# Weight sums, paired tiles, index arithmetic and the end of a switch: one regrouping in a mixture-of-experts stage

## The chip, the cores and the metric

The kernel runs on one core of one Trainium2 chip. The metric is the device time of a run in microseconds (us). A core has TensorE (PE) for products, VectorE (DVE), ScalarE (ACT) and GpSimd (POOL) for elementwise work, and SyncE (SP), which here starts the transfers of weights. Each engine takes its instructions in order from its own queue; engines wait for one another through semaphores. GpSimd also starts the gathers and scatters by index (DMA_INDIRECT).

## The reference

Two blocks follow one another. The first is a banded attention with position bias (4 sequences, 8 heads, 768 positions, 64 per head); the change doesn't touch it. The second routes each of the 3072 tokens to the best of 8 experts:

```python
N, D, E, F = (3072, 512, 8, 1024)
logits = x @ w_gate
expert_idx = np.argmax(logits, axis=1)
gate_w = probs[np.arange(N), expert_idx]      # softmax of the logits
for e in range(E):
    mask = expert_idx == e
    h = np.maximum(x[mask] @ w1[e], 0.0)
    out[mask] = gate_w[mask, None] * (h @ w2[e])
```

All values are float32.

## The kernel before

**The parts.** Attention and routing fill about the first 200 us. They write each token with its gate weight and number to a row of its expert in DRAM (`xs_dram`). Then come the experts, class `Experts`, called from `passes`, one expert after another. Within an engine, instructions stand in the order in which the code calls them (`manual_schedule`); the program only adds the semaphores.

**The tokens of an expert.** 256 tokens are computed as two tiles of 128 (`xg`, transposed to `xT`). Experts 0 and 1 have another full tile computed before the loop (`up_s`, `down_s`). What is left of an expert's tokens comes from `xs` and is computed in a *form*: `units(e, k)`. The form number k, 0 to 7, is known only at run time, and says which of three tiles are there: a big one of 128 tokens, a middle one of 64, a low one of 32. `tc.Switch` (L1187) branches to the code of the form on TensorE, ScalarE and VectorE and back behind it. `hint` (L1180) tells TensorE and ScalarE early where the branch will go. In this run expert 0 has a middle and a low tile, 1 and 7 a low one, 2 and 4 a big one, 3, 5 and 6 a big and a low one.

**Seven products in place of eight.** The 256 tokens are multiplied by a scheme in the manner of Strassen and Winograd: both operands are cut in 2x2 blocks, sums of blocks are formed, and seven block products replace eight. So there are four sums of weight blocks for w1 (`combine1`, tile `c1`, 128x1024 each), four for w2 (`combine2`, tile `c2`, 128x1024 each), four of the tokens (`x_combine`, tile `cx`), and sums of the hidden values (`h`, `ch`) and of the results (`UV`, `gu`, `y`). The trace calls c1 and c2 both `c`.

**One expert, in order.** Inside the form: the transposes of the remainder tiles (L1124 big, L1131 smaller) are copied by VectorE to `xsT` (L1125, L1135), and TensorE does `up_a(e, 0)`, the first four of the seven block products for chunk 0 of four chunks of hidden units. `up_sums(0)` adds partial results out of PSUM bank `u[0]`: a copy on ScalarE (L1029), a sum on VectorE (L1030). Then come the remainder's products (L1144 small, `up_s` at L853 big), `up_a` and `up_sums` of chunk 1, `up_b(0)` (the other three products of chunk 0, which are added on top in the same bank, so the bank must have been read by `up_sums` first), and the remainder's second layer (L861 big, L1168 small).

Behind the form: `gather_u` and `send_u` on GpSimd, then `up_a`, `up_b`, `up_sums` and `up_end` of the remaining chunks. `up_end(j)` makes the seven tiles that the second layer needs of chunk j. Then `down_a` and `down_b` (L1066, L1075), with the next expert's `combine1` on VectorE under them, `x_in` (transposes L999 of the next expert's tokens, copies L1000 on VectorE and L1001 on ScalarE), `x_combine`, and the scaled outputs `y_out`. The last things before the next form are `combine_w2(e + 1)` (one sum on VectorE, L976, three on GpSimd, L974, L975, L977) and `meta_u(e + 1)` (L1106 to L1110, VectorE: gate weights and token numbers of the remainder, as tiles of 128x3). For two experts, `judge` puts a few more small operations there; for expert 2 it reads a result from bank `t[0]`, where the next transposes go (L1279).

**Weights** are fetched two experts ahead by SyncE into two buffers (`w[e % 2]`).

## Time and profile before

| | |
|---|---|
| Time, median of 3 runs | 636.07 us (634.67 to 636.08) |
| Profiled execution | 632.8 us |
| Mean granted clock of TensorE | 0.93 |
| Experts loop, from the first form to the last product | about 216 to 613 us |
| TensorE busy, 303.6 to 346 us (expert 2) | 30.0 of 42.4 us, granted clock 0.84 |
| TensorE busy, 390 to 417 us | 25.7 of 27 us, granted clock 1.00 |

Parts of the profile speak of different things. The busy line gives each engine's share of the span. The waits say which engine stood idle before which line, and what ended the idle time. The timeline lists instructions in order of time: start, duration, engine, line, operation, tiles, and in brackets the idle time before. The windows give busy time in stretches, with the clock that TensorE was granted (PEclk, a share of full speed). A branch isn't listed in the timeline, and the time it takes stands as idle time that "issue" ended.

### The profile page before, as it was taken

What the parts mean: (1) busy time and instruction counts of PE and PEld (TensorE: products, weight loads), DVE (VectorE), ACT (ScalarE), POOL (GpSimd) and SP (SyncE); (2) the same over time, 40 slices, a digit from 0 to 9 for tenths busy, and PEclk for the clock granted to TensorE, in tenths of its full rate; (3) what the DMA queues carried; (4) which work ended last, traced back from release to release, by engine and by line L of the source; (5) the groups of instructions that cost most, each with busy time, mean ns of one, the idle gap of its engine ahead of it and who ended that gap; (6) DMA issues with size and microseconds to landing.
All of it is one profiled execution on the core that took longest, in us unless ns stands there. A gap on an engine that the chain in (4) does not pass through costs nothing. (4 is left out here: it accounts for less than half of the span.)

```text
span 632.8 us, 13136 instructions
## 1 busy us (share of the span) xinstructions
PE 528.5 (84%) x5329; PEld 443.3 (70%) x5329; DVE 337.3 (53%) x796; ACT 139.9 (22%) x286; POOL 202.8 (32%) x204
## 2 busy tenths in 40 slices
PE   6899899899899889679389689959959995996870
PEld 5788688688687559559287576947948784794860
DVE  5567467458556426918714921870781394176330
ACT  3645254254321111102011111201211110020110
POOL 4201401401405741750811522180181134135110
PEclk9999999899899989989789979989988997997995
DMA  9989899899403304515403601540451261000000
GB/s 184 205 186 232 231 250 224 232 242 210 151 3 106 119 4 160 169 53 201 144 19 106 212 35 34 201 145 26 156 179 35 80 218 68 11 20 36 6 35 3
DMA packets 99342, 78.04 MB, mean 123 GB/s; under 512 B 80054, under 2 KB 80056, under 8 KB 99200
## 3 DMA queue, kind: packets, MB, share of 16 engines
q1 hardware_dynamic: 90368, 56.63, 35.0%
q0 software_dynamic: 8000, 19.77, 9.2%
q8 instruction: 56, 0.92, 0.6%
q14 instruction: 86, 0.70, 0.4%
q10 hardware_dynamic: 832, 0.02, 0.1%
HBM read 63.54 MB, written 14.73 MB: 124 GB/s over the span
## 5 line engine op out<-in xcount | busy, mean ns | idle before, releaser
L372 DVE TENSOR_TENSOR p<-sp,other 128x1024 f32<-128x1024 f32 x40 | 47.5, 1221 | 50.6 <-PE sp L358 48.7
L1030 DVE TENSOR_TENSOR uv<-uv,u 128x256 f32<-128x256 f32 x32 | 13.4, 419 | 110.8 <-ACT uv L1029 100.8
L853 PE MATMUL d<-xsT,w 128*128 128x128 f32 x320 | 42.3, 300 | 19.9 <-DVE xsT L1125 19.9
L853 PEld LDWEIGHTS d<-xsT,w 128*128 128x128 f32 x320 | 41.4, 215 | 22.3 <-DVE xsT L1125 20.3
L785 POOL DMA_INDIRECT xg<-xs_dram,grow x16 | 24.4, 1524 | 88.1 <-issue 84.2
L1144 PE MATMUL u<-w,xsT 128*32 128x256 f32 (+1 forms) x208 | 23.4, 566 | 31.5 <-DVE xsT L1135 31.5
L861 PE MATMUL d<-w,hsT 128*128 128x512 f32 x112 | 49.6, 593 | 0.1
L1023 PE MATMUL u<-cx,c 128*128 128x128 f32 x384 | 48.8, 277 | 0.0
L1066 PE MATMUL d<-c,ch 128*128 128x256 f32 x192 | 46.7, 379 | 0.0
L1023 PEld LDWEIGHTS u<-cx,c 128*128 128x128 f32 x384 | 46.3, 195 | 0.0
L1029 ACT COPY uv<-u 128x256 f32<-128x256 f32 x32 | 11.9, 372 | 151.3 <-PE u L1023 145.3
L379 ACT ACTIVATE p<-p 128x1024 f32<-128x1024 f32 (+1 forms) x48 | 44.6, 977 | 2.1 <-DVE p L372 2.0
L358 PE MATMUL sp<-qt,kt 64*128 64x128 f32 x448 | 41.3, 293 | 1.2 <-DVE kt L244 1.2
L300 POOL COPY ka<-kt 128x384 f32<-128x384 f32 x16 | 8.2, 510 | 105.8 <-DVE den_all L423 102.8
L785 POOL DMA_INDIRECT xs<-xs_dram,grow x24 | 24.3, 1014 | 54.1 <-PE d L853 37.1
L1066 PEld LDWEIGHTS d<-c,ch 128*128 128x128 f32 x192 | 36.5, 190 | 5.0
L1144 PEld LDWEIGHTS u<-w,xsT 128*32 128x32 f32 (+1 forms) x208 | 8.8, 151 | 43.0 <-DVE xsT L1135 32.5
L387 PE MATMUL po<-p,vt 128*64 128x128 f32 x448 | 37.1, 274 | 0.0
L861 PEld LDWEIGHTS d<-w,hsT 128*128 128x128 f32 x112 | 20.6, 190 | 23.4 <-issue 23.4
L358 PEld LDWEIGHTS sp<-qt,kt 64*128 64x128 f32 x448 | 34.1, 204 | 3.3 <-ACT qt L242 1.6
L398 PE MATMUL pr<-p,one_in 128*32 128x128 f32 x704 | 28.5, 278 | 8.7 <-issue 7.9
L793 POOL DMA_INDIRECT out_dram<-ys,to_u x8 | 8.2, 1019 | 78.7 <-DVE yu L1171 46.9
(238 smaller groups left out, 1138.3 us busy)
## 6 DMA issues: line engine op xcount, KB each, us to landing
w<-in_moe_w_dram SPq DMA_DIRECT2D x24, 1024.0 KB, 5.0
w<-in_moe_w_dram SPq DMA_DIRECT2D x16, 512.0 KB, 6.3
raw_q<-in_q_dram SPq DMA_DIRECT2D x24, 256.0 KB, 4.6
raw_k<-in_k_dram SPq DMA_DIRECT2D x24, 256.0 KB, 4.4
vt<-in_v_dram SPq DMA_DIRECT2D x24, 256.0 KB, 5.8
va<-vt SPq DMA_DIRECT2D x16, 192.0 KB, 5.6
va<-vt SPq DMA_DIRECT2D x16, 64.0 KB, 5.2
xs_dram<-xr,slot_i POOLq DMA_INDIRECT x24
```

Source lines behind the costliest of these rows:

```text
L358: nc.tensor.matmul(sp[:, a, j, t, :], lhsT=kt[r, m, :], rhs=qts[n][r, m, :], start=True, stop=True, skip_group_check=True)
L372: nc.vector.tensor_tensor(z, sc, bi, ALU.add)
L379: nc.scalar.activation(z, z, AF.Exp)
L387: nc.tensor.matmul(po[D * a:D * a + D, m, :], lhsT=vt[:, 2 * m + a, :], rhs=ps[n][m // 2][:, a, m % 2, t, :], start=(x == 0), stop=(x == l ...
L398: nc.tensor.matmul(pr[GW * m:GW * m + GW, 0, :], lhsT=one_in[:, a, :], rhs=ps[n][m // 2][:, a, m % 2, t, :], start=(x == 0), stop=False, s ...
L785: nc.gpsimd.indirect_dma_start(out=dst.bitcast(I32), out_offset=None, in_=xs_dram[:], in_offset=bass.IndirectOffsetOnAxis(ap=idx, axis=0), ...
L853: nc.tensor.matmul(ph[:, i, :], lhsT=self.w[e % 2][0][:, c, ts(half * HF + i, P)], rhs=xT[:, c, :], start=(c == 0), stop=(c == NDC - 1), s ...
L861: nc.tensor.matmul(py[:].rearrange("p a b -> p (a b)"), lhsT=self.hsT[:, f, :], rhs=self.w[e % 2][1][:, f, :], start=(f == 0), stop=(f == ...
L1023: nc.tensor.matmul(self.u[j][:, r, :], lhsT=lhs(k), rhs=rhs(k), start=first, stop=True, skip_group_check=True)
L1030: nc.vector.tensor_tensor(uv[:], uv[:], self.u[j][:, 2:4, :], ADD)
L1066: nc.tensor.matmul(self.half(i, j), lhsT=lhs, rhs=rhs, start=(f == 0 and j == 0), stop=True, skip_group_check=True)
L1144: nc.tensor.matmul(ph[n * g:n * g + n, :], lhsT=xm[:, c, cols[s]], rhs=w1t[:, c, ts(g, m)], start=(c == 0), stop=(c == NDC - 1), skip_grou ...
```

## The change

Five things are regrouped in the experts' loop; the same sums and products are computed.

1. All four sums of w2 blocks go to VectorE and to other places: three into the expert's own form (behind `up_sums(0)` and `up_b(0)`), the fourth under `down_a`. `combine_w2` at the end of the expert before is gone.
2. The sums of hidden values are done for pairs of chunks in one operation (`up_22`, `h_combine`), for which `h`, `ch` and `uv` are laid out anew; the order of operations in the scheme changes a little with it.
3. The index work is moved to GpSimd: `meta_u`, and the token numbers and gates in `x_in`.
4. Chunk 2's first products and sums (`up_a(e, 2)`, `up_sums(2)`) move from behind the form to its end.
5. Copies out of PSUM change engines: the big remainder tile and both halves of `xT` are copied by ScalarE. The scaling `gated` is split off `down_sums` and comes after `x_in`. Two of `x_combine`'s sums become one operation.

The core of the diff:

```diff
         def combine2(self, e):
-            w = self.w[e % 2][1]
-            return list(self.right([self.c2[:, i] for i in range(4)], ...
-        def combine_w2(self, e):
-            c = self.combine2(e)
-            c[2](nc.vector)
-            for i in (0, 1, 3):
-                c[i](nc.gpsimd)
+            yield lambda: nc.vector.tensor_tensor(c[:, 0], b12, b11, SUB)
+            yield lambda: nc.vector.tensor_tensor(c[:, 1], b22, c[:, 0], SUB)
+            yield lambda: nc.vector.tensor_tensor(c[:, 2], b12, b22, SUB)
+            yield lambda: nc.vector.tensor_tensor(c[:, 3], b21, c[:, 1], SUB)
...
         def x_in(self, e):
-            nc.vector.tensor_copy(out=self.xT[:, :, 0:P], in_=self.t[0][:])
-            nc.scalar.copy(self.xT[:, :, P:2 * P], self.t[1][:])
-            nc.vector.tensor_tensor(self.to[e % 2][:], ... ALU.bitwise_or)
-            nc.vector.tensor_copy(out=self.gate[e % 2][:], in_=self.xg[:, :, DM])
+            for t in range(2):
+                nc.scalar.copy(self.xT[:, :, ts(t, P)], self.t[t][:])
+            nc.gpsimd.tensor_tensor(self.to[e % 2][:], ... ADD)
+            nc.gpsimd.tensor_copy(out=self.gate[e % 2][:], in_=self.xg[:, :, DM])
...
+        def up_22(self, i):
+            j, h = slice(2 * i, 2 * i + 2), self.h[:, 2]
+            nc.vector.tensor_tensor(h[:, j, :], self.uv[:, j, 0, :], self.uv[:, j, 1, :], ADD)
+            nc.scalar.activation(h[:, j, :], h[:, j, :], AF.Relu)
         def up_end(self, j):
-            nc.vector.tensor_tensor(h[:, 1:3, :], ... b[:, 1:4:2, :], ADD)
-            nc.vector.tensor_scalar(h[:, 0, :], b[:, 0, :], 0.0, None, MAX)
-            nc.scalar.activation(h[:, 2, :], h[:, 2, :], AF.Relu)
-            nc.vector.scalar_tensor_tensor(c[:, 0, :], h[:, 1, :], 0.0, h[:, 3, :], MAX, ADD)
-            nc.vector.tensor_tensor(c[:, 1, :], c[:, 0, :], h[:, 0, :], SUB)
-            nc.vector.scalar_tensor_tensor(c[:, 2, :], h[:, 1, :], 0.0, h[:, 0, :], MAX, SUB)
-            nc.vector.tensor_tensor(c[:, 3, :], h[:, 2, :], c[:, 1, :], SUB)
+            nc.vector.tensor_tensor(self.h[:, 1:4:2, j, :], ... b[:, 1:4:2, :], ADD)
+            nc.vector.tensor_scalar(self.h[:, 0, j, :], b[:, 0, :], 0.0, None, MAX)
+        def h_combine(self, i):
+            nc.scalar.activation(h[:, 1], h[:, 1], AF.Relu)
+            nc.vector.scalar_tensor_tensor(h[:, 4], h[:, 3], 0.0, h[:, 2], MAX, ADD)
+            nc.vector.scalar_tensor_tensor(c[:, 0:2], h[:, 3:5], 0.0, ... MAX, SUB)
+            nc.vector.tensor_tensor(c[:, 2], h[:, 1], c[:, 1], SUB)
...
         def units(self, e, k):
-                nc.vector.tensor_copy(out=self.xsT[0][:], in_=self.t[0][:])
+                nc.scalar.copy(self.xsT[0][:], self.t[0][:])
...
             self.up_sums(0)
+            next(c2)()
...
             self.up_sums(1)
+            self.up_22(0)
...
             self.up_b(e, 0)
+            next(c2)()
+            next(c2)()
...
+            self.up_a(e, 2)
+            self.up_sums(2)
...
         def passes(self, judge):
                 self.send_u(e)
-                self.up_a(e, 2)
-                self.up_sums(2)
                 self.up_b(e, 1)
                 self.up_end(0)
+                self.up_end(1)
+                self.h_combine(0)
                 self.up_a(e, 3)
                 self.up_sums(3)
+                self.up_22(1)
                 self.up_b(e, 2)
-                for j in (1, 2):
-                    self.up_end(j)
+                self.up_end(2)
                 self.up_b(e, 3)
                 self.up_end(3)
+                self.h_combine(1)
                 self.down_a(e)
+                list(self.combine2(e))[3]()
...
-                    self.combine_w2(e + 1)
                     self.meta_u(e + 1)
```

`meta_u` is the same arithmetic on GpSimd, with the conversion to whole numbers as an operation of its own.

More of the change, by code (lines that the diff above doesn't have):

```diff
@@ L877, in begin @@
             self.cx = T([P, 4, HD, P], "cx")
-            self.h = T([P, HF, 4, P], "h")
-            self.ch = T([P, HF, 4, P], "ch")
-            self.uv = [T([P, 2, P], f"uv{i}") for i in range(HF)]
+            self.h = T([P, 5, HF, P], "h")
+            self.ch = T([P, 3, HF, P], "ch")
+            self.uv = T([P, HF, 2, P], "uv")
             self.UV = T([P, 2, HM], "UV")
@@ L970, in combine1 @@
             yield lambda: nc.vector.tensor_tensor(c[:, 3], a12, c[:, 1], SUB)
-        def right(self, c, b11, b12, b21, b22, sign=1):
-            yield lambda eng: eng.tensor_tensor(c[0], b12, b11, SUB)
-            yield lambda eng: eng.tensor_tensor(c[1], b22, c[0], SUB)
-            yield lambda eng: eng.tensor_tensor(c[2], *((b22, b12) if sign > 0 else (b12, b22)), SUB)
-            yield lambda eng: eng.tensor_tensor(c[3], b21, c[1], SUB)
-        def combine2(self, e):
-            w = self.w[e % 2][1]
-            return list(self.right([self.c2[:, i] for i in range(4)],
-                                   *(w[:, HF * k:HF * k + HF, HM * j:HM * j + HM]
-                                     for k in range(2) for j in range(2)), sign=-1))
-        def combine_w2(self, e):
-            c = self.combine2(e)
-            c[2](nc.vector)
-            for i in (0, 1, 3):
-                c[i](nc.gpsimd)
+        def combine2(self, e):
+            w, c = self.w[e % 2][1], self.c2
+            b11, b12, b21, b22 = (w[:, HF * k:HF * k + HF, HM * j:HM * j + HM]
+                                  for k in range(2) for j in range(2))
+            yield lambda: nc.vector.tensor_tensor(c[:, 0], b12, b11, SUB)
+            yield lambda: nc.vector.tensor_tensor(c[:, 1], b22, c[:, 0], SUB)
+            yield lambda: nc.vector.tensor_tensor(c[:, 2], b12, b22, SUB)
+            yield lambda: nc.vector.tensor_tensor(c[:, 3], b21, c[:, 1], SUB)
         def gather_x(self, e):
@@ L999, in x_in @@
                     nc.tensor.transpose(self.t[t][:, c, :], self.xg[:, t, ts(c, P)], ident[:])
-            nc.vector.tensor_copy(out=self.xT[:, :, 0:P], in_=self.t[0][:])
-            nc.scalar.copy(self.xT[:, :, P:2 * P], self.t[1][:])
-            nc.vector.tensor_tensor(self.to[e % 2][:], self.xg[:, :, DM + 1].bitcast(I32),
-                                    self.inv_i[:, e, :], ALU.bitwise_or)
-            nc.vector.tensor_copy(out=self.gate[e % 2][:], in_=self.xg[:, :, DM])
-        def x_combine(self):
-            for fn in self.right([self.cx[:, i] for i in range(4)],
-                                 *(self.xT[:, HD * k:HD * k + HD, P * j:P * j + P]
-                                   for k in range(2) for j in range(2))):
-                fn(nc.vector)
@@ L1014, in up_a @@
-        def up_a(self, e, j):
-            w, c = self.w[e % 2][0], self.c1
-            f = ts(j, P)
-            first = True
-            for r, lhs, rhs in ((0, lambda k: w[:, k, f], lambda k: self.xT[:, k, 0:P]),
-                                (2, lambda k: c[:, 1, k, f], lambda k: self.cx[:, 1, k, :]),
-                                (1, lambda k: c[:, 0, k, f], lambda k: self.cx[:, 0, k, :]),
-                                (3, lambda k: c[:, 2, k, f], lambda k: self.cx[:, 2, k, :])):
+            for t in range(2):
+                nc.scalar.copy(self.xT[:, :, ts(t, P)], self.t[t][:])
@@ new lines, in x_in @@
+            nc.gpsimd.tensor_tensor(self.to[e % 2][:], self.xg[:, :, DM + 1].bitcast(I32),
+                                    self.inv_i[:, e, :], ADD)
+            nc.gpsimd.tensor_copy(out=self.gate[e % 2][:], in_=self.xg[:, :, DM])
+        def x_combine(self):
+            x, c = self.xT, self.cx
+            nc.vector.tensor_tensor(c[:, 0:2], x[:, :, P:2 * P].rearrange("p (k c) t -> p k c t", k=2),
+                                    x[:, 0:HD, :].rearrange("p c (j t) -> p j c t", j=2), SUB)
+            nc.vector.tensor_tensor(c[:, 2], x[:, HD:NDC, P:2 * P], c[:, 0], SUB)
+            nc.vector.tensor_tensor(c[:, 3], x[:, HD:NDC, 0:P], c[:, 2], SUB)
@@ L1022, in up_a, with products @@
+        def products(self, bank, terms, first):
+            for r, lhs, rhs in terms:
                 for k in range(HD):
-                    nc.tensor.matmul(self.u[j][:, r, :], lhsT=lhs(k), rhs=rhs(k), start=first, stop=True,
+                    nc.tensor.matmul(bank[:, r, :], lhsT=lhs(k), rhs=rhs(k), start=first, stop=True,
                                      skip_group_check=True)
                     first = False
-        def up_sums(self, j):
-            uv = self.uv[j]
-            nc.scalar.copy(uv[:], self.u[j][:, 0:2, :])
-            nc.vector.tensor_tensor(uv[:], uv[:], self.u[j][:, 2:4, :], ADD)
-            nc.vector.tensor_tensor(self.h[:, j, 3, :], uv[:, 0, :], uv[:, 1, :], ADD)
-            nc.scalar.activation(self.h[:, j, 3, :], self.h[:, j, 3, :], AF.Relu)
@@ L1034, in up_b, with up_a @@
-        def up_b(self, e, j):
-            w, c = self.w[e % 2][0], self.c1
-            f, f2 = ts(j, P), ts(HF + j, P)
-            for r, lhs, rhs in ((0, lambda k: w[:, HD + k, f], lambda k: self.xT[:, HD + k, 0:P]),
-                                (1, lambda k: c[:, 3, k, f], lambda k: self.xT[:, HD + k, P:2 * P]),
-                                (3, lambda k: w[:, HD + k, f2], lambda k: self.cx[:, 3, k, :])):
-                for k in range(HD):
-                    nc.tensor.matmul(self.u[j][:, r, :], lhsT=lhs(k), rhs=rhs(k), start=False, stop=True,
-                                     skip_group_check=True)
+        def up_a(self, e, j):
+            w, c, x, f = self.w[e % 2][0], self.c1, self.xT, ts(j, P)
+            self.products(self.u[j], (
+                (0, lambda k: w[:, k, f], lambda k: x[:, k, 0:P]),
+                (3, lambda k: c[:, 0, k, f], lambda k: self.cx[:, 0, k, :]),
+                (1, lambda k: c[:, 2, k, f], lambda k: self.cx[:, 1, k, :]),
+                (2, lambda k: c[:, 1, k, f], lambda k: self.cx[:, 2, k, :])), True)
@@ new lines, in up_b @@
+        def up_b(self, e, j):
+            w, c, x, f = self.w[e % 2][0], self.c1, self.xT, ts(j, P)
+            self.products(self.u[j], (
+                (0, lambda k: w[:, HD + k, f], lambda k: x[:, HD + k, 0:P]),
+                (3, lambda k: c[:, 3, k, f], lambda k: x[:, HD + k, P:2 * P]),
+                (1, lambda k: w[:, HD + k, ts(HF + j, P)], lambda k: self.cx[:, 3, k, :])), False)
+        def up_sums(self, j):
+            uv = self.uv[:, j]
+            nc.scalar.copy(uv, self.u[j][:, 0:2, :])
+            nc.vector.tensor_tensor(uv, uv, self.u[j][:, 2:4, :], ADD)
@@ L1044, in up_end @@
+        def up_22(self, i):
+            j, h = slice(2 * i, 2 * i + 2), self.h[:, 2]
+            nc.vector.tensor_tensor(h[:, j, :], self.uv[:, j, 0, :], self.uv[:, j, 1, :], ADD)
+            nc.scalar.activation(h[:, j, :], h[:, j, :], AF.Relu)
         def up_end(self, j):
-            h, c, b = self.h[:, j], self.ch[:, j], self.u[j]
-            nc.vector.tensor_tensor(h[:, 1:3, :], self.uv[j][:, 0:1, :].to_broadcast([P, 2, P]),
+            b = self.u[j]
+            nc.vector.tensor_tensor(self.h[:, 1:4:2, j, :], self.uv[:, j, 0:1, :].to_broadcast([P, 2, P]),
@@ new lines, in h_combine @@
+        def h_combine(self, i):
+            h, c = (t[:, :, 2 * i:2 * i + 2, :].rearrange("p q j t -> p q (j t)") for t in (self.h, self.ch))
+            nc.scalar.activation(h[:, 1], h[:, 1], AF.Relu)
+            nc.vector.scalar_tensor_tensor(h[:, 4], h[:, 3], 0.0, h[:, 2], MAX, ADD)
+            nc.vector.scalar_tensor_tensor(c[:, 0:2], h[:, 3:5], 0.0,
+                                           h[:, 0:1].to_broadcast([P, 2, 2 * P]), MAX, SUB)
+            nc.vector.tensor_tensor(c[:, 2], h[:, 1], c[:, 1], SUB)
@@ L1061, in down_a @@
             for f in range(HF):
-                for i, j, lhs, rhs in ((0, 0, self.h[:, f, 0, :], w[:, f, 0:HM]),
-                                       (0, 1, self.ch[:, f, 0, :], self.c2[:, 0, f, :]),
-                                       (1, 0, self.ch[:, f, 1, :], self.c2[:, 1, f, :]),
-                                       (1, 1, self.ch[:, f, 2, :], self.c2[:, 2, f, :])):
+                for i, j, lhs, rhs in ((0, 0, self.h[:, 0, f, :], w[:, f, 0:HM]),
+                                       (0, 1, self.h[:, 4, f, :], self.c2[:, 0, f, :]),
+                                       (1, 0, self.ch[:, 1, f, :], self.c2[:, 1, f, :]),
+                                       (1, 1, self.ch[:, 0, f, :], self.c2[:, 2, f, :])):
                     nc.tensor.matmul(self.half(i, j), lhsT=lhs, rhs=rhs, start=(f == 0 and j == 0),
@@ L1070, in down_b @@
             w = self.w[e % 2][1]
-            for i, j, lhs, rhs in ((0, 1, lambda f: self.ch[:, f, 3, :], lambda f: w[:, HF + f, HM:DM]),
-                                   (0, 0, lambda f: self.h[:, f, 2, :], lambda f: w[:, HF + f, 0:HM]),
-                                   (1, 1, lambda f: self.h[:, f, 3, :], lambda f: self.c2[:, 3, f, :])):
+            for i, j, lhs, rhs in ((0, 1, lambda f: self.ch[:, 2, f, :], lambda f: w[:, HF + f, HM:DM]),
+                                   (0, 0, lambda f: self.h[:, 1, f, :], lambda f: w[:, HF + f, 0:HM]),
+                                   (1, 1, lambda f: self.h[:, 2, f, :], lambda f: self.c2[:, 3, f, :])):
                 for f in range(HF):
@@ L1081, in down_sums, with gated @@
             nc.vector.tensor_tensor(flat(self.UV), flat(self.UV), flat(self.d[1]), ADD)
+        def gated(self, e):
             for t in range(2):
@@ L1105, in meta_u @@
             f = self.to_f
-            nc.vector.tensor_copy(out=f[:], in_=self.xs[:, :, DM + 1].bitcast(I32))
+            nc.gpsimd.tensor_copy(out=f[:], in_=self.xs[:, :, DM + 1].bitcast(I32))
             for i in (1, 2):
-                nc.vector.tensor_scalar(f[:, i:i + 1], f[:, i:i + 1], float(2 * i), None, MUL)
-            nc.vector.tensor_tensor(self.to_u[e % 2][:], f[:], self.inv_u[:, e, :], ADD)
-            nc.vector.tensor_copy(out=self.gate_u[e % 2][:], in_=self.xs[:, :, DM])
+                nc.gpsimd.tensor_scalar(f[:, i:i + 1], f[:, i:i + 1], float(2 * i), None, MUL)
+            nc.gpsimd.tensor_tensor(f[:], f[:], self.inv_u[:, e, :], ADD)
+            nc.gpsimd.tensor_copy(out=self.to_u[e % 2][:], in_=f[:])
+            nc.gpsimd.tensor_copy(out=self.gate_u[e % 2][:], in_=self.xs[:, :, DM])
         def send_u(self, e):
@@ L1116, in units @@
         def units(self, e, k):
+            c2 = self.combine2(e)
             big, mid, low = k >> 2, k >> 1 & 1, k & 1
@@ L1211, in passes @@
                     self.x_in(e + 1)
+                self.gated(e)
                 self.down_b(e)
@@ L1269 @@
         ex.scatter(ex.ys[1][:], ex.tos[:, 1:2])
-        ex.combine_w2(0)
         ex.meta_u(0)
```

## The prediction

> **What bounds the kernel now.** I read the page for the busy shares, then TensorE's waits, then the timeline around one of them, then the granted clock there.

> ```profile
> span 632.8 us, 13136 instructions
> PE 528.5 (84%) x5329; PEld 443.3 (70%) x5329; DVE 337.3 (53%) x796; ACT 139.9 (22%) x286; POOL 202.8 (32%) x204
> ```

> TensorE is the bound: 84% busy. The chain of waits holds only the last scatter and explains nothing, so the question is what TensorE's missing 16% waits for. Its waits from 205 us on (engine, line, releaser: total us, times, longest):

> ```profile
> PE u L1144 <- DVE xsT L1135: 31.5, 5, 7.9
> PE d L853 <- DVE xsT L1125: 19.9, 2, 12.3
> PE t L1124 <- issue: 8.4, 2, 8.1
> PE u L1023 <- issue: 5.0, 3, 2.9
> ```

> Some 60 us are lost at one place: the start of each of the eight forms, before the first product that needs a transposed remainder tile copied by VectorE. In the timeline the gaps are 4.04, 6.91, 12.35, 8.09, 7.58, 7.87, 6.58, 6.14 = 59.6 us for experts 0 to 7. Expert 3's is named "issue", but the transposes there wait for bank t0, which VectorE reads for L1279 behind the same work. Expert 6's start (start, duration, engine, line):

> ```profile
> 519.51 0.48 DVE L1093 SCALAR_TENSOR_TENSOR y<-d,gate,gu 128x256 f32<-128x256 f32 x1 [0.38 <-PE d L1075]
> 519.91 2.80 DVE L976 TENSOR_TENSOR c<-w 128x1024 f32<-128x1024 f32 x1
> 521.69 3.21 POOL L975 TENSOR_TENSOR c<-w,c 128x1024 f32<-128x1024 f32 x1
> 522.63 2.30 DVE L1106 CAST to_f<-xs 128x3 f32<-128x3 int32 x1
> 524.98 2.34 POOL L977 TENSOR_TENSOR c<-w,c 128x1024 f32<-128x1024 f32 x1
> 525.21 2.13 DVE L1109 TENSOR_TENSOR to_u<-to_f,inv_u 128x3 int32<-128x3 f32 x1
> 528.41 0.69 DVE L1125 COPY xsT<-t 128x512 f32<-128x512 f32 x1 [1.00 <-issue]
> 529.02 0.28 DVE L1135 COPY xsT<-t 128x128 f32<-128x128 f32 x1
> 529.36 3.21 PE L1144 MATMUL u<-w,xsT 128*32 128x256 f32 x28 [6.58 <-DVE xsT L1135]
> ```

> Between the last y (519.5) and the copy (528.4) VectorE does 8.5 us of combine_w2 and meta_u, most of it inflated: the sum takes 2.80 where its likes at L967 to L970 take 1.22, and a 128x3 cast 2.30 where it took 0.155 once. Each inflated operation lies beside a GpSimd sum. After a gap the products are slow too (busy us, then PEclk):

> ```profile
> 318.05:322.55 4.50, 4.50 (x21) 4.50 (x22) 0.56 (x2) 0.31 (x1) 1.84 (x2) 0.50 0.01 0
> 322.55:327.40 4.85, 4.85 (x45) 4.85 (x45) 0.00 (x0) 0.60 (x1) 0.16 (x1) 1.00 0.08 22
> ```

> Half the clock for 4.5 us after expert 2's gap. The last view is VectorE crossing a form's edge:

> ```profile
> 553.16 0.35 DVE L1171 TENSOR_SCALAR yu<-u,gate_u 128x128 f32<-128x128 f32 x1 [1.24 <-PE u L1168]
> 556.18 0.42 DVE L1030 TENSOR_TENSOR uv<-uv,u 128x256 f32<-128x256 f32 x1 [2.67 <-ACT uv L1029]
> 578.61 0.42 DVE L1110 COPY gate_u<-xs 128x3 f32<-128x3 f32 x1
> 582.06 0.29 DVE L1135 COPY xsT<-t 128x128 f32<-128x128 f32 x1 [3.02 <-issue]
> ```

> Leaving a form, 3.0 us pass from the start of its last operation to the next one, though ScalarE's copy ended at 555.6. Entering one, 3.4 us pass where nothing else runs over it (3.55 idle at expert 2). The hint is for TensorE and ScalarE alone (L1181).

> [...] gaps of 2.91 and 1.96 us (before L1023 at 282.7 and 593.3) were followed by full speed, one of 4.04 was not.

> **The change, part by part.** I follow one expert from X, the end of the last product of its form, to the first waiting product of the next form. TensorE's own steps at full clock, start to start: up_a 1.79, up_b 1.34, down_a 6.91, x_in's transposes 0.87, down_b 5.20, each set of xs transposes 0.4.

> Form exit. up_a(2) and up_sums(2) are now in front of VectorE's branch. up_a(2) ends X+1.8, ScalarE's copy (0.37) X+2.2, the sum starts there, and 3.0 later, at X+5.2, VectorE goes on. Then up_end(0) and up_end(1), 0.54 each (spacing of L1047 to L1051): X+6.3. h_combine(0): a 256-wide operation (0.41), a 512-wide (0.69, as L1081) and a 256-wide (0.41), with small waits: X+7.8. Only then up_sums(3) reads bank u3, until X+8.2, and up_b(3) writes it. TensorE reaches up_b(3) at X+6.3 and waits 2.0 us: a **new wait**, in which its own exit stall (0 to 2.9 today) vanishes.

> Second half. up_b(3) ends X+9.6; up_22(1), up_end(2), up_end(3), h_combine(1) end X+11.9. down_a (X+9.6 to 16.5) needs pair 1 at X+13.1: no wait. The weight sum c2[3] and three of combine1, 1.2 each, end X+16.6, hidden under down_a. ScalarE's two copies of xT (0.56 each, L1001) end X+18.0, the gated ones (0.91) X+18.9; then y_out 0.45, x_combine 0.69+0.41+0.41, combine1's last 1.2, two y's 0.8: the last y starts X+22.8, while down_b ends X+22.5. The c2 sum and meta_u, 8.5 us here, are gone from this place.

> Form entry. TensorE finishes transposes and up_a(0) at X+24.8. A form with a big tile alone now takes its copy from ScalarE, which ran ahead: it goes on at once, X+24.8. A form with a small tile needs VectorE, at X+22.8+3.4, plus a 0.3 copy and 0.2 of signalling: X+26.7, a wait of 1.9. Expert 3 waits for L1279 first: X+27.1.

> Inside. c2's other sums come behind the first up_sums and after up_b(0), under 2 to 7 us of products; up_22(0) ahead of the hu copy (0.42) delays forms without a big tile by 0.3: 1 us in all. GpSimd's eight tiny operations have no row; up to 0.3 each (memsets of 128x256: 0.22) they hide in its waits of 12 to 15 us[...]. The other regrouping of h and ch is in the chain above; weights are fetched during earlier experts.

> Intervals from X, measured and after, by next expert: 1, 30.2 to 26.7; 2, 38.3 to 24.8; 3, 33.7 to 27.1; 4, 31.6 to 24.8; 5, 31.6 to 26.7; 6, 30.9 to 26.7; 7, 29.4 to 26.7; the tail 22.1 to 21.7. That is 3.5+13.5+6.6+6.8+4.9+4.2+2.7+0.4 = 42.6. At expert 0 the copy comes at 220.5 instead of 222.6+0.6: 2.6. Sum 45.2.

> Clock. With waits of 2 us I expect full speed. Lost today to the half clock inside forms, as duration less that of the same group at full speed: 1.6 (expert 0), 2.3, 2.4 (9.39 against 7.03 for 64 products), 2.3 (expert 4), 2.4, 2.5, 1.4 = 14.9; expert 3's is in its interval.

> 45.2 + 14.9 - 1 = 59: 636 - 59 = **577 us**.

> **The rivals.** First, *half the clock remains*. [...] For: 4.04 us sufficed. Against: 2.91 did not. All 14.9 lost again and 0.5 us more per form edge of VectorE (16 x 0.5): 577+15+8 = 600. Second, *VectorE crosses sooner*. Three entries today showed only about 1.0 us of idle time, but there the inflated casts covered the branch, which speaks against it. Without the new wait (8 x 2.0), 561. Third, **slower**: TensorE's own branches stop being hidden. For: the forms grow by 32 TensorE instructions each, and before L1023 there is a stall of 2.9 today. Against: only two of eight exits show more than a microsecond. If all 16 crossings cost 3.8 us more (the longest branch record on TensorE), 577+61 = 638.

> **How the numbers follow.** Main case 0.62, the first rival 0.20, the second 0.10, the third 0.06, no difference by some cancelling 0.02. So faster 0.92, same 0.02, slower 0.06. The low end takes in the second rival, the high end the first and the unknown edges: 561 to 601.

> **What would show it.** TensorE's waits for xsT at L1135/L1144's place fall to about 2 us each, those at the big copy to nothing; a new wait of TensorE before up_b(3) of some 2 us, ended by VectorE's up_sums(3); no 2 us casts on tiny tiles; weight sums of 1.22 everywhere; VectorE's first operation after a form about 3 us behind up_sums(2); granted clock near 1.00 through the experts. I am wrong if the clock still drops at form starts, if TensorE waits longer than 3 us at a form's edge, or if a GpSimd step holds a gather that TensorE then waits for.

## The result, and the profile after

| | before | after |
|---|---|---|
| Time, median of 4 runs | 635.78 us | 595.25 us (589.79 to 600.11) |
| Ratio to before | | 0.9337, 95% interval 0.9273 to 0.9401 |
| Profiled execution | 632.8 us | 588.0 us |
| Mean granted clock | 0.930 | 0.969 |

The change is 40.5 us faster, where 59 us were forecast; 595.25 lies inside the range, 18 us above the forecast. Ratios, here and below, are of the fast runs alone, those within 1.5% of the fastest of the same kernel (600.11 is left out here). The busy shares of the kernel after:

```profile
span 588.0 us, 12952 instructions
PE 520.6 (89%) x5329; PEld 437.1 (74%) x5329; DVE 301.5 (51%) x647; ACT 139.4 (24%) x267; POOL 152.1 (26%) x244
```

TensorE does the same 5329 products in a shorter span. GpSimd lost 50 us of work (202.8 to 152.1). TensorE's waits from 205 us on (line numbers have moved: L1010 holds all of `up_a` and `up_b`, L1149 is the small remainder's first layer, L1035 the sum of `up_sums`):

```profile
PE u L1010 <- DVE uv L1035: 15.4, 8, 2.5
PE u L1149 <- DVE xsT L1139: 12.8, 6, 3.1
PE u L1010 <- ACT uv L1034: 1.1, 1, 1.1
PE t L1128 <- issue: 0.9, 1, 0.9
```

The 59.6 us ahead of the forms have become 12.8, all of it at small tiles (0.9 more, in the last line, stands ahead of expert 3's transposes); the wait at the big copy is gone. A new wait stands in the first line: 8 times, about 1.9 us each, one per expert. In the timeline, expert 6's exit from its form shows where it comes from:

```profile
515.19 0.42 DVE L1035 TENSOR_TENSOR uv<-uv,u 128x256 f32<-128x256 f32 x1 [2.00 <-ACT uv L1034]
518.00 0.42 DVE L1044 TENSOR_TENSOR h<-uv,u 128x256 f32<-128x256 f32 x1 [2.39 <-issue]
519.51 0.69 DVE L1052 SCALAR_TENSOR_TENSOR ch<-h 128x512 f32<-128x512 f32 x1
520.65 0.41 DVE L1035 TENSOR_TENSOR uv<-uv,u 128x256 f32<-128x256 f32 x1
521.12 0.71 PE L1010 MATMUL u<-xT,w 128*128 128x128 f32 x4 [1.91 <-DVE uv L1035]
```

VectorE's sum (515.2) is the last thing in front of its branch; 2.8 us later it goes on, works through `up_end` and `h_combine(0)`, and reads bank u3 only at 520.65. TensorE has stood before `up_b(3)` for 1.91 us. The other edge, the entry into the same form:

```profile
484.83 0.47 DVE L1095 SCALAR_TENSOR_TENSOR y<-d,gate,gu 128x256 f32<-128x256 f32 x1
489.49 0.29 DVE L1139 COPY xsT<-t 128x128 f32<-128x128 f32 x1 [4.18 <-issue]
489.84 3.49 PE L1149 MATMUL u<-w,xsT 128*32 128x256 f32 x32 [2.45 <-DVE xsT L1139]
```

After the last y nothing stands in front of the branch any more, but from the start of that operation to the copy 4.66 us pass, where I had taken 3.4. The windows tell what is different (busy us of each engine, then PEclk, DMA share, GB/s). The first and the last are entries that took 3.4 and 2.9 us, of experts 2 and 7; between them are those of experts 5 and 6:

```profile
299.33:302.75 3.42, 3.42 (x33) 3.42 (x33) 0.00 (x0) 0.00 (x0) 2.51 (x3) 1.00 0.71 238
433.17:438.27 5.10, 2.50 (x22) 2.18 (x20) 0.42 (x2) 0.96 (x2) 2.11 (x2) 1.00 0.80 295
484.88:489.34 4.46, 2.50 (x22) 2.18 (x20) 0.43 (x2) 0.96 (x2) 2.10 (x2) 1.00 0.88 319
535.97:538.89 2.92, 2.06 (x18) 1.86 (x16) 0.43 (x2) 0.37 (x1) 2.03 (x2) 1.00 0.23 93
```

The two long entries are those with the most traffic, though not in proportion: 5.10 us goes with 295 GB/s and 4.46 with 319. In the kernel before, expert 6's branch fell into a stretch with 6 GB/s, and 2.9 us passed from it to the first instruction of the form. Last, the clock at the products behind expert 6's wait, and just after:

```profile
489.84:493.05 3.21, 3.21 (x32) 1.38 (x32) 1.41 (x2) 0.00 (x0) 0.00 (x0) 0.50 0.07 25
493.30:500.60 7.30, 7.30 (x69) 7.30 (x66) 0.00 (x0) 0.98 (x2) 0.47 (x1) 1.00 0.01 3
```

A wait of 2.45 us did bring a stretch of half clock.

### The profile page after: what moved, and what is told of

It reads as the page before. It is cut to its first block, busy times and chain, and to the rows that moved or that the text cites. A ratio compares the mean times of both kernels' runs of the same rounds, so it can differ in the third digit from the quotient of the medians.

```text
span 588.0 us, 12952 instructions
## 1 busy us (share of the span) xinstructions
PE 520.6 (89%) x5329; PEld 437.1 (74%) x5329; DVE 301.5 (51%) x647; ACT 139.4 (24%) x267; POOL 152.1 (26%) x244
## 5 line engine op out<-in xcount | busy, mean ns | idle before, releaser
L1010 PE MATMUL u<-xT,w 128*128 128x128 f32 x256 | 42.0, 287 | 16.8 <-DVE uv L1035 15.4
L1035 DVE TENSOR_TENSOR uv<-uv,u 128x256 f32<-128x256 f32 x32 | 13.3, 417 | 78.3 <-ACT uv L1034 66.0
L1010 PEld LDWEIGHTS u<-xT,w 128*128 128x128 f32 x256 | 34.2, 193 | 22.7 <-DVE uv L1035 16.9
L1010 PE MATMUL u<-cx,c 128*128 128x128 f32 x384 | 48.1, 275 | 0.0
L1010 PEld LDWEIGHTS u<-cx,c 128*128 128x128 f32 x384 | 45.5, 192 | 0.0
L785 POOL DMA_INDIRECT xg<-xs_dram,grow x16 | 18.9, 1184 | 89.7 <-PE t L990 82.6
L785 POOL DMA_INDIRECT xs<-xs_dram,grow x24 | 24.8, 1033 | 57.1 <-PE d L853 36.5
L853 PEld LDWEIGHTS d<-xsT,w 128*128 128x128 f32 x320 | 36.1, 192 | 1.7 <-issue 1.7
L853 PE MATMUL d<-xsT,w 128*128 128x128 f32 x320 | 36.9, 276 | 0.0
L1066 PE MATMUL d<-c,ch 128*128 128x256 f32 x128 | 33.6, 386 | 0.0
L398 PEld LDWEIGHTS pr<-p,one_in 128*32 128x32 f32 x704 | 19.3, 110 | 15.7 <-issue 13.9
L1149 PE MATMUL u<-w,xsT 128*32 128x256 f32 (+1 forms) x208 | 19.4, 496 | 12.8 <-DVE xsT L1139 12.8
```

The source lines that it names most:

```text
L398: nc.tensor.matmul(pr[GW * m:GW * m + GW, 0, :], lhsT=one_in[:, a, :], rhs=ps[n][m // 2][:, a, m % 2, t, :], start=(x == 0), stop=False, s ...
L785: nc.gpsimd.indirect_dma_start(out=dst.bitcast(I32), out_offset=None, in_=xs_dram[:], in_offset=bass.IndirectOffsetOnAxis(ap=idx, axis=0), ...
L853: nc.tensor.matmul(ph[:, i, :], lhsT=self.w[e % 2][0][:, c, ts(half * HF + i, P)], rhs=xT[:, c, :], start=(c == 0), stop=(c == NDC - 1), s ...
L1010: nc.tensor.matmul(bank[:, r, :], lhsT=lhs(k), rhs=rhs(k), start=first, stop=True, skip_group_check=True)
L1035: nc.vector.tensor_tensor(uv, uv, self.u[j][:, 2:4, :], ADD)
L1066: nc.tensor.matmul(self.half(i, j), lhsT=lhs, rhs=rhs, start=(f == 0 and j == 0), stop=True, skip_group_check=True)
```

## The experiments

Each was run beside the kernel before on the same chip. The sets differ in the attention part (mean clock of the first 198 us 0.97 in some, 1.00 in the others; the kernel before takes 636 or 620 us), so I compare ratios and differences to the kernel before of the same set. It takes 636 us in the first set (the change) and in that of e5 to e8, and 620 in those of e1 to e4 and of e9 to e12. Several of the texts below, written ahead, put the difference down to the chip; the record gives e1 to e4 and e5 to e8 the same chip number, so its cause isn't known. Absolute times expected for e1 to e4 are meant for 636 us.

| Run | Ratio to before, 95% interval | us less than before (medians of all runs) |
|---|---|---|
| the change (first set) | 0.9337 (0.9273 to 0.9401) | 40.5 |
| e5 the change again | 0.9351 (0.9316 to 0.9387) | 40.2 |
| e1 only the sums and meta_u moved | 0.9300 (0.9206 to 0.9395) | 39.5 |
| e10 sums on VectorE, in place | 1.0025 (1.0002 to 1.0049) | -1.2 |
| e12 the change, meta_u on VectorE | 0.9387 (0.9312 to 0.9462) | 32.1 |
| e2 the change, filler products | 0.9352 (0.9288 to 0.9416) | 39.1 |
| e4 the change, hint for VectorE | 0.9310 (0.9242 to 0.9378) | 42.2 |
| e6 the change, no weight transfers | 0.9117 (0.9083 to 0.9152) | 55.0 |
| e3 the change, first products back | 0.9107 (0.9022 to 0.9191) | 54.0 |
| e7 the change, small copy on ScalarE | 0.9065 (0.9034 to 0.9096) | 59.3 |
| e8 e3 and e7 together | 0.8851 (0.8817 to 0.8886) | 72.1 |
| e9 e1 and both copies on ScalarE | 0.8772 (0.8747 to 0.8797) | 75.4 |
| e11 e7, only up_sums(2) behind the form | 0.8654 (0.8633 to 0.8676) | 82.2 |

### The change again: e5

**e5** is the changed kernel itself, unedited, so that the runs of its set have it beside them on the same chip.

> The changed kernel unaltered, as the common base of this set of runs and of the runs before it, whose chip gave the kernel before a shorter time (619.6 us). If that difference lies outside the experts (in the attention, before 180 us), its ratio to the kernel before is 0.930 to 0.940 again and its time about 578 us when the kernel before takes 620.

Measured: 595.67 us (593.62 to 597.15) where the kernel before took 635.84. The ratio repeats that of the first set. In this set, too, the kernel before takes 636 us. Its four runs spread by 3.5 us, those of the first set by 10.3.

### Which part of the change carries it: e1, e10, e12

**e1** moves the sums of w2 blocks and meta_u in the kernel before, and nothing else.

```diff
             self.up_sums(0)
+            c2[0](nc.vector)
...
             self.up_b(e, 0)
+            c2[1](nc.vector)
+            c2[2](nc.vector)
...
                 self.down_a(e)
+                self.combine2(e)[3](nc.vector)
...
-                    self.combine_w2(e + 1)
```

> The kernel before with two edits alone: the four sums of w2 blocks on VectorE at the places that the change gives them, and meta_u on GpSimd. Tiles of h and ch, the copies, and chunk 2's first products stay as before. Theory A (the gain is the work that stood on VectorE ahead of the next form, and the half clock that its wait caused): TensorE's waits for xsT fall from about 60 us to 8 waits of 2 to 3.5 us, big forms included since their copy is still VectorE's; no wait before up_b(3); 585 to 597 us, as good as the whole change (595). Theory B (pairs of chunks in one operation and chunk 2's products inside the form carry part of it): the gain is clearly smaller than the whole change's, 605 us or more.

Measured: 580.11 us where the kernel before took 619.63. Its waits:

```profile
PE u L1147 <- DVE xsT L1136: 15.0, 6, 3.5
PE d L853 <- DVE xsT L1126: 8.2, 2, 4.5
PE u L1023 <- issue: 6.6, 4, 2.6
```

Theory A holds: the moved work alone gives what the whole change gives (39.5 against 40.2 and 40.5 us; the ratio 0.930 lies where 585 to 597 us of 636 do, 0.920 to 0.939). There is no wait before `up_b(3)`; there is one of 8.2 us at the big copy, which is VectorE's here. So what the rest of the change won at one place it lost at another, and the next runs say where.

**e10** leaves the place and takes GpSimd away from it. It also gives VectorE the three sums that GpSimd did there.

```diff
             c[2](nc.vector)
             for i in (0, 1, 3):
-                c[i](nc.gpsimd)
+                c[i](nc.vector)
```

> The kernel before with one edit: combine_w2's three GpSimd sums run on VectorE, at the same place ahead of the next form. Theory A (what costs is the place: VectorE's queue ahead of its branch, with the branch of 3.0 to 3.4 us now uncovered behind short operations): ahead of the form 4 sums of 1.22, meta_u's 0.8 and the branch make 9 us where 9.5 are today; 626 to 636 us, 0.985 to 1.00 of the kernel before. Theory B [...]: the inflated 2.8 and 2 x 2.1 us fall to 1.22 and 0.3, three sums of 1.22 are added, and with them eight waits shorten by 2 to 3 us, half-clock time too: 0.97 or less.

Measured: 621.85 us against 620.65; the ratio's interval, 1.0002 to 1.0049, leaves no gain. Expert 6's entry on VectorE:

```profile
503.75 1.22 DVE L976 TENSOR_TENSOR c<-w 128x1024 f32<-128x1024 f32 x1
507.40 1.23 DVE L977 TENSOR_TENSOR c<-w,c 128x1024 f32<-128x1024 f32 x1
508.54 0.16 DVE L1106 CAST to_f<-xs 128x3 f32<-128x3 int32 x1
508.99 0.16 DVE L1109 TENSOR_TENSOR to_u<-to_f,inv_u 128x3 int32<-128x3 f32 x1
512.16 0.69 DVE L1125 COPY xsT<-t 128x512 f32<-128x512 f32 x1 [2.94 <-issue]
```

The inflation is gone (1.22 in place of 2.80, 0.16 in place of 2.30 and of 2.13), and nothing is won: from the first sum to the copy 8.4 us pass, as the 8.5 before. Two things fill the 5.7 us that the inflation took: three more sums of 1.22 on VectorE, 3.7 us, and 1.9 us of the branch, which the inflated casts had been covering (idle time before the copy 2.94 in place of 1.00). So the run doesn't price the inflation by itself. It shows that the work has to leave this place, whichever engine does it; e1 shows that this is enough.

**e12** puts meta_u back on VectorE in the changed kernel (the five operations as before).

> The changed kernel with meta_u back on VectorE. Theory A (any operation there delays VectorE's branch, and six forms have a small tile that waits for it): five tiny operations, 0.8 to 0.9 us, added to six waits, with more half-clock windows: 4 to 10 us slower than the changed kernel, 0.941 to 0.951 of the kernel before. Rival [...]: 0.932 to 0.938, as the changed kernel.

Measured: 0.9387, interval 0.9312 to 0.9462. It holds the rival's numbers, half of theory A's and the changed kernel's ratio. The ratio rests on two of the four runs (580.41 and 587.98 us); with the other two (589.21 and 590.83) the median is 588.60, 0.948 of the kernel before, which would speak for theory A. What the move of the index work is worth on its own stays open, from nothing to some 8 us.

### The wait before up_b(3): e3

**e3** puts chunk 2's first products and their sums back behind the form.

```diff
             # end of units
-            self.up_a(e, 2)
-            self.up_sums(2)
...
                 self.send_u(e)
+                self.up_a(e, 2)
+                self.up_sums(2)
                 self.up_b(e, 1)
```

> The changed kernel with up_a(2) and up_sums(2) back behind the form. Theory A (inside the form they hold VectorE's branch back by 2.4 us, and that is the new wait before up_b(3)): TensorE's waits there, 15.4 us in all, vanish; its own exit from the form shows again where the branch takes 2 to 4 us: 5 to 12 us in all; 583 to 590 us. Rival (the place inside the form is what hides TensorE's exits): waits of 2 to 3.5 us after five or more forms, 593 to 600 us.

Measured: 565.64 us against 619.63, 54.0 us less, where the change had 40.

```profile
PE u L1149 <- DVE xsT L1139: 15.8, 6, 3.7
PE u L1010 <- issue: 6.0, 3, 2.5
PE u L1010 <- DVE uv L1035: 0.4, 1, 0.4
```

The wait for `up_sums(3)` falls from 15.4 to 0.4 us, and TensorE's own exits come back with 6.0, in three forms. Theory A holds: this part of the change costs 14 us, a quarter of the 54 that the rest gains.

### The entry into the form: e6, e7, e4

**e6** leaves out the weight transfers of experts 2 to 7 (`self.fetch(e + 2)` removed); those experts compute with the weights of experts 0 and 1.

> The changed kernel without the weight transfers inside the experts' loop; experts 2 to 7 compute with the weights of experts 0 and 1, so the values differ and the work is the same. Theory A (VectorE's entry into a form, 4.3 to 5.1 us at experts 4 to 6 where 3.4 was expected, is stretched by the weight transfers that now run at 313 to 382 GB/s at the same moment): all entries 2.8 to 3.4 us, TensorE's waits for xsT 1.3 to 2.1 each, and 5 to 9 us faster than the changed kernel in this set. Rival (the entry's length follows the position in the code): entries of experts 4 to 6 stay at 4.3 us or more, same time within 2 us.

Measured: 55.0 us less than before, 14.8 less than the changed kernel in the same set (580.85 against 595.67). From VectorE's branch to its first instruction in the form, experts 1 to 7: 2.8, 3.3, 2.8, 2.8, 2.9, 2.8, 2.8 us; in the changed kernel in this set 4.7, 3.3, 6.6, 4.5, 4.9, 4.6, 2.7 (at expert 7, the last, no weights are on the way in either kernel). The windows of experts 5 and 6, to be read against the 5.10 and 4.46 us above:

```profile
430.73:433.65 2.92, 2.50 (x22) 2.18 (x20) 0.43 (x2) 0.96 (x2) 2.11 (x2) 1.00 0.24 95
480.65:483.43 2.78, 2.50 (x22) 2.18 (x20) 0.43 (x2) 0.84 (x2) 2.03 (x2) 1.00 0.26 103
```

Theory A holds: the weight transfers stretch the entry. The waits for xsT fall from 15.0 to 5.5 us; the rest of the 14.8 goes with fewer stretches of half clock (three in the experts in the profiled run, against seven; mean clock 0.973 over the four runs, against 0.960). That is more than the 5 to 9 us expected, since I had left the clock out.

In VectorE's branch the prediction saw only idle time; the DMA's records show more. From expert 5's branch (433.17) to VectorE's first instruction in the form (438.27), exactly one packet (of 8 KB) of the queue named "instruction" is recorded in the change, within 436.35 to 436.75 us. In e6, where the branch lies at 430.73 and the instruction at 433.65, one is recorded within 431.80 to 432.30:

```profile
q14 instruction: 1, 0.01, 4.8%
q14 instruction: 1, 0.01, 4.5%
```

It begins 3.23 us behind the branch in the change and 1.1 to 1.6 us behind it in e6; from there to the instruction 1.87 and 1.3 to 1.9 us pass. In each of the 16 entries of the change and of the kernel before, such a packet begins 1.6 to 2.3 us before that instruction. So at expert 5 the time that is longer with the weight transfers is the one up to the start of this packet. Which engine the packet belongs to, and whether the branch waits for it, the record doesn't say.

**e7** lets ScalarE, which is hinted, copy the small tile as well.

```diff
-                nc.vector.tensor_copy(out=xm[:, :, r], in_=self.t[1][:, :, r])
+                nc.scalar.copy(xm[:, :, r], self.t[1][:, :, r])
```

> The changed kernel with the copy of the small remainder tile on ScalarE too, in place of VectorE. Theory A (VectorE's branch into the form is what TensorE waits for there): no wait for xsT longer than 0.3 us (12.8 us in the changed kernel), fewer half-clock windows, 12 to 18 us faster than the changed kernel. Rival (the time moves on to the next thing that VectorE owes after its entry, the sum that up_b(0) waits for, or the hu copy): the waits reappear at up_b(0) or at L1176 and less than 5 us is won.

Measured: 576.50 us against the change's 595.67 in the same set, 19.2 us less, a little more than expected. Theory A holds.

```profile
PE u L1010 <- DVE uv L1035: 16.3, 9, 2.4
PE t L1128 <- issue: 0.9, 1, 0.9
PE u L1176 <- DVE hu L1162: 0.3, 2, 0.2
```

No wait for xsT is left. VectorE still enters late (one entry took 7.3 us), but what it owes inside the form isn't needed for several microseconds.

**e4** gives VectorE the hint (`self.ENGINES` in place of `self.ENGINES[:2]`).

> The changed kernel with the branch hint given to VectorE too. Theory A (the 1.4 to 3.1 us waits of small remainder products are VectorE's unhinted entry into the form, 3 to 5 us from its branch to its first operation): the entry falls below 0.5 us, TensorE's waits for xsT (12.8 us in all) fall below 2 us, fewer half-clock windows: 577 to 585 us. Rival (VectorE reaches the branch too late or the hint doesn't reach it in time): entry 3 us as before, within 2 us of the changed kernel.

Measured: 0.9310, not to be told from the change. Two entries, experts 2 and 5, fell to 0.5 us; those of experts 4 and 6 took 5.9 and 6.5, and TensorE's waits for xsT are 11.7 us, while those that end with VectorE's sums (L1035) are 19.0 where the change has 15.4. Neither theory as stated: the hint works at times. Why not always stays open. Taking the work away from the engine was the surer way.

### The clock: e2

**e2** fills TensorE's two waits with 12 products of the identity each, results unused.

```diff
+            for i in range(12 if small else 0):
+                nc.tensor.matmul(self.u[2][:, 0, :], lhsT=ident[:], rhs=ident[:], ...)
             for s in small:
...
+                for i in range(12):
+                    nc.tensor.matmul(self.t[1][:, 0, :], lhsT=ident[:], rhs=ident[:], ...)
                 self.up_b(e, 3)
```

> The changed kernel with 12 products of the identity by itself (about 0.11 us each, results unused) put into TensorE's two waits: ahead of the small remainder's first products (1.4 to 3.1 us of wait there) and ahead of up_b(3) (2 to 2.5 us). Theory A (what the prediction missed, 595 for 577, is to a good part half-clock windows that the remaining 2 to 3 us waits cause, and the spread of 590 to 600 us too): granted clock about 0.98 and no half-clock window in the experts, 585 to 589 us, runs within 2 us of each other. Rival (the missing part is longer waits for VectorE's branches, and the clock follows chance): time within 2 us of the changed kernel, 593 to 597, and the spread stays; or slower by up to 10 us if the fillers lengthen the path.

Measured: the clock part came as theory A has it, 1.00 through the experts, and runs from 579.49 to 581.67, a spread of 2.2 us where the change had 10.3 and, in e5, 3.5. (Four runs are few to judge a spread: e7, with stretches of half clock, has 2.7.) The time is that of the change (0.9352). I had mis-sized the fillers:

```profile
L1145 PE MATMUL u<-ident x144: 275/275/276, 202.0 to 526.5; 128*128 128x128 f32 x144
L1217 PE MATMUL t<-ident x192: 274/275/276, 226.1 to 543.6; 128*128 128x128 f32 x192
```

Each of these products stands in the trace as two records, 144 and 192 for 72 and 96 products, so a group of 12 takes 2.7 us and not 1.3. Fourteen groups are 38 us, with 4.0 us of waits left, in place of the 28 us of waits that they fill. The time should have grown by about 14 us and didn't, so the full clock gave back about as much. This is worked out and not measured apart: half clock costs the changed kernel something like 10 to 15 us. The clock's record gives about as much: the profiled run of the change has four stretches of 3.41 us within the experts, that of e5 seven, and each costs at most half its length, 1.7 us, so 7 and 12 us; e2 has none. The changed kernel's own runs go the same way: 589.79 us at a clock of 0.969, 595.73 at 0.958, 600.11 at 0.953.

Which waits are hit can be read from the traces. In the profiled run of the change, every stretch of half clock begins a whole number of times 3.41 us behind the first one (13, 26, 55, 100, 106, 121 and 146 times); in that of the kernel before it is 13, 26, 43, 56 and so on, up to 158. I call the windows of 3.41 us so counted a grid. Four windows of this grid in the change, at experts 0 and 6, and two in the kernel before, at expert 1's exit (the first time behind the comma is TensorE's busy time; the clock stands behind the busy times):

```profile
240.46:243.87 3.41, 1.51 (x14) 1.32 (x12) 2.82 (x8) 0.68 (x2) 0.00 (x0) 1.00 0.82 307
243.87:247.29 3.42, 3.26 (x21) 3.05 (x22) 2.65 (x8) 0.83 (x2) 0.00 (x0) 1.00 0.16 23
486.22:489.63 3.41, 1.16 (x11) 0.97 (x9) 0.14 (x1) 0.37 (x1) 1.21 (x2) 1.00 0.78 296
489.63:493.05 3.42, 3.21 (x32) 1.39 (x32) 1.61 (x3) 0.00 (x0) 0.00 (x0) 0.50 0.07 26
278.18:281.59 3.41, 1.58 (x60) 1.31 (x48) 0.35 (x1) 0.00 (x0) 1.03 (x1) 1.00 0.04 12
281.59:285.01 3.42, 2.35 (x21) 2.36 (x22) 0.00 (x0) 0.27 (x1) 1.97 (x2) 1.00 0.10 27
```

Expert 0's wait of 2.06 us left 1.90 us of one window idle, and the next had the full clock. Expert 6's of 2.45 us left 2.25 us idle, and the next had half. The 2.91 us in the kernel before lay across two windows, 1.83 and 1.07 us idle, and brought no half clock. Over these two profiled runs, 207 windows of their grids between 198 us and the last product have the full clock. Each of the 12 with 2.10 us or more idle was followed by half the clock, and none of the 195 with 1.91 or less. That is a count of these windows and no rule: in the attention of the change, the window from 117.58 us was idle for 1.48 us and was followed by half the clock.

### Put together: e8, e9, e11

**e8** has the edits of e3 and e7.

> The changed kernel with the small copy on ScalarE and with up_a(2) and up_sums(2) back behind the form. Theory A (the two waits are independent): the gains add, 25 to 32 us faster than the changed kernel, about 547 to 553 us on a chip where the kernel before takes 620; what is left of waits is TensorE's own exit from forms, about 6 us. Rival (both waits come from one lag of VectorE, which then shows elsewhere): less than 20 us faster.

Measured: 563.71 us against 595.67, 32.0 us less than the change: the gains, 14 (e3, in its own set) and 19, add. The ratio, 0.885, is 549 us where the kernel before takes 620. What is left is TensorE's exit from the forms:

```profile
PE u L1010 <- issue: 7.1, 4, 3.1
PE t L1128 <- issue: 0.9, 1, 0.9
```

**e9** is e1 with both copies on ScalarE: h and ch by single chunks, `x_combine` in four operations, `x_in` as in the kernel before.

> The kernel before with the sums of w2 blocks and meta_u moved as in the change, chunk 2's first products left behind the form, and the copies of both remainder tiles, big and small, on ScalarE. It differs from the kernel with both edits (0.885 of the kernel before) only in the layout of h and ch by single chunks, in x_combine and in the copies of xT. Theory A (pairs of chunks in one operation and the split of gated are worth nothing, since VectorE isn't what TensorE waits for there): 0.880 to 0.892 of the kernel before. Theory B (they are worth the 2% by which the kernel with only the work moved, 0.930, lies behind the one with first products back, 0.911): 0.90 or more.

Measured: 0.8772, 75.4 us less than before, against 0.8851 and 72.1 of e8, in another set. It came out a little better than theory A's range, which holds: pairs of chunks in one operation, the joint operation in `x_combine`, the split of `gated` and the edits in `x_in` together bring nothing that can be seen. The distance between e1 and e3 is then probably for the most part the big copy on ScalarE, whose wait of 8.2 us in e1 is none in e3; no run moves that copy alone.

**e11** takes up both findings: `up_a(2)` stays at the end of the form, where it covers TensorE's exit, and `up_sums(2)` goes behind it, where it doesn't hold VectorE's branch back.

```diff
             self.up_a(e, 2)
-            self.up_sums(2)
...
                 self.send_u(e)
+                self.up_sums(2)
                 self.up_b(e, 1)
```

> The changed kernel with the small copy on ScalarE, and with chunk 2's first products (up_a(2)) left inside the form but their sums (up_sums(2)) behind it. Theory A (TensorE's exit needs its products inside the form, VectorE's branch must not wait for their sums): TensorE's stalls at the exit (7.1 us with both behind) fall below 3 us and the wait before up_b(3) stays below 3 us in all; 556 to 561 us, 0.875 to 0.883 of the kernel before. Rival (VectorE's branch still ends too late for up_sums(2), and up_b(2) or up_b(3) waits): 563 to 570 us.

Measured: 538.45 us (538.01 to 539.54) where the kernel before took 620.65, ratio 0.8654: the best version, 82 us less than before where the change has 40, and better than the 0.875 to 0.883 of theory A. Its waits and busy share:

```profile
PE u L1010 <- ACT uv L1034: 1.4, 2, 0.8
PE t L1128 <- issue: 0.9, 1, 0.9
PE u L1010 <- DVE uv L1035: 0.4, 1, 0.4
PE u L1176 <- DVE hu L1162: 0.3, 2, 0.2
PE 503.9 (94%) x5329; PEld 428.7 (80%) x5329; DVE 299.6 (56%) x641; ACT 141.8 (26%) x273; POOL 154.5 (29%) x244
```

Some 3 us of waits remain behind 190 us, TensorE is busy for 94% of the span, and the profiled run has no stretch of half clock in the experts.

## Why the prediction was right, and where it was short

**The place of the loss** was right: 59.6 us ahead of the forms, and e1 shows that moving the work away from there gives the whole net gain of the change.

**The cause within it** was half right. I read the inflation beside GpSimd's sums (2.80 us, where the sum's likes take 1.22) as part of the cost. e10 shows that without it the place costs the same (8.4 us against 8.5), since the sums then take VectorE's time and the branch lies bare. The forecast moved the sums away and did count that branch (3.4 us), so its sum wasn't hurt.

**Form exit and the new wait**: right in mechanism and size. Forecast 8 waits of 2.0 us before `up_b(3)`, ended by `up_sums(3)`; measured 8 and 15.4 us. VectorE was to go on at X+5.2; at expert 6 X is 512.7 and it went on at 518.0, X+5.3.

**Big tiles** and the tiny operations: right. The wait at the big copy is gone. GpSimd's tiny operations take 0.2 us, those of L1110 (128x1) up to 1.05, and TensorE waits for none of them.

**Form entry** is the first step that failed. I took 3.4 us, from VectorE's last operation ahead of the form to the copy, from the two bare entries of the kernel before, experts 2 and 7. The change enters forms while the weights for a later expert are under way, and at experts 1, 3, 5 and 6 it took 4.5, 4.5, 5.3 and 4.7 us (3.1 at expert 7). The waits for xsT came to 2.8, 3.1 and 2.5 us at experts 1, 5 and 6, forecast 1.9. Over all, the intervals from the end of a form to the first waiting product of the next were forecast at 205 us with the tail, and measured at 216 in the profiled run. Of these 11 us some 5 are the longer entries and 1.7 a stretch of half clock under expert 4's `down_a`. The other 4 are small: VectorE's last y came 0.4 to 0.9 us later than at X+22.8, half clock apart, and the tail took 1.1 more. The forecast's 0.2 us of signalling was an estimate; from the end of the small copy to the product 0.05 to 0.06 us pass, in both profiles.

**Clock** is the second. "With waits of 2 us I expect full speed" was wrong, since it judged a wait by its length: in the profile waits of 2.84, 3.10 and 2.45 us at experts 1, 5 and 6 were followed by half-clock stretches, and one of 2.31 us before expert 4's `up_b(3)` by a stretch within its `down_a`. Behind the first three waits the small products took 3.1, 3.4 and 3.5 us where 1.9 is the full-speed duration, 4.3 us in all. With the 11 us above, that is a little more than the 13 us by which the profiled run missed 577. Which waits are hit differs from run to run, and the profiled run was the fastest of the four; the median lies 5.5 us above it. The first rival named half clock behind the waits, and gave it all the weight or none; it happens in part. The windows shown under e2 tell how the kernel before could have 2.91 us without a stretch of half clock and the change 2.45 us with one.

**The number** lies inside the range because the range took in the first rival: 595 is nearer to its 600 than to 577. Two of the signs of being wrong that I had named came true: the clock dropped at three form starts, and one wait, at expert 5, was longer than 3 us (3.10).

## What to carry to other kernels

Where an engine branches at run time, count the branch as an operation in its queue: here 2.8 to 3.3 us without weight transfers (e6), and up to 6.6 with them (e5). Let the work that others wait for at the edge run on an engine that got there early, and put nothing that waits for another engine just in front of the branch. Before believing that a slow operation is the cost, ask what it hides and what would stand there without it: here the inflated casts covered part of a branch (idle time before the copy 1.00 us with them, 2.94 without). And where waits of some 2 us or more remain, look at the clock behind each of them: in the change it was half behind waits of 2.31, 2.45, 2.84 and 3.10 us, and full behind others of 2.06 and 2.46.
